# Decayed attention and a leaky-ReLU MLP on one core: loads of v on a second queue, more buffers for q, k and v, and a new order of all work

## The chip, the cores and the metric

The kernel runs on 1 core of one Trainium2 chip. The metric is device time in microseconds (us) of one execution; the median of the runs is given with the lowest and the highest. The engines are named as in the profile: PE (TensorE matmul), PEld (its weight loads), DVE (VectorE), ACT (ScalarE), POOL (GpSimd) and SP (SyncE, which only issues DMAs here). Each engine takes its instructions in the order in which they were written; engines wait for each other by semaphores.

## The reference

```python
# q, k, v: float32 [8 batches, 8 heads, 576 positions, 64]
scores = q @ k^T / sqrt(64)
gamma  = 1 - 2 ** (-5 - head)
ret    = scores * (gamma ** (i - j) where i >= j, else 0)
x      = (ret @ v), heads side by side     # [4608 tokens, 512]
h      = x @ w_in                          # [4608, 2048]
out    = max(0.01 * h, h) @ w_out          # [4608, 512], float32
```

## The kernel before

**Units and groups.** The 4608 tokens are 36 units of 128 tokens (`u` = 0 to 35), and four units make a group of 512 tokens (`g` = 0 to 8). The attention is done in linear form over chunks of 64 positions: a state (a sum of k^T v, with decay) is carried from chunk to chunk, so that a unit needs only its own scores and the state before it. Everything behind the loads is fp16 with float32 sums in PSUM.

**The jobs of a unit.** Each piece of work has a name:

- `ld{u}.1`, `ld{u}.0`, `ld{u}.2`: the loads of k, q and v, 256 KB each (L335 to L346), into `t32_1`, `t32_0`, `t32_2`; each of the three has `ld` = 4 buffers
- `ck`, `cq`, `cv`: casts to fp16, q and v with a decay factor (L364 to L385), into `qk16` and `v16`
- `tp{u}.x` with `yt{u}.x` (units 0 to 7): transposes of k (x = 1) and q (x = 0) on PE and their copy out of PSUM; `tr{u}` (units 8 to 35): the transpose of both by a DMA on SP's queue (L387 to L396). Both fill `qkT`
- `sb`: k^T v of the two chunks; `st{u}.j`: its sum into the state (DVE, an `s` at the end of the name for the step with decay); `sx`: the state's cast to fp16
- `sa`, `mk`: the scores and their masking on DVE; `oa` (units 0 to 3) or `ca` and `ow` (later ones, `ca` holding the scores too): the output's matmuls; `x{u}`: its copy into `xT`

**The MLP.** `h{g}.{f}.{t}` are the plain products of layer 1 for groups 0 and 1 (f: first of the 128-wide column blocks, t: first token), `l...` the leaky ReLU behind them. One such job is 4 to 16 matmuls. For groups 2 to 8, layer 1 is four sets `a{g}.{n}` of seven block products each instead of eight, and layer 2 is `b{g}` with seven products `p1` to `p7`, each in two parts (`seven`, L736). Their sums on other engines are `cA`, `u2`, `k5` (copies out of PSUM) and `11`, `12`, `21`, `22` (results). `xs`, `m`, `ws` and `wm` are sums of inputs and of weights on DVE, `so` the stores of the results. The four quarters of `w_in` (`wi0` to `wi3`) and of `w_out` (`wo0` to `wo3`) are cast to fp16 by the DMA that loads them, always on POOL's queue.

**The order.** `ORDER` (L113) is one list of all jobs. `Plan.emit` (L44) writes them out in that order, so it fixes each engine's own order and that of the DMA queues: SP's queue issues the loads of its units, the transposes and the stores in the order in which they stand there, and POOL's queue its loads. `@n` says which of four PSUM banks a product takes. `+n@b` (`filler`, L970) puts n idle products of 512 columns on PE. `ENGINE` (L82) says whether a cast or a copy runs on DVE or on ACT. `CFG["loads"]` (L71) says which queue loads a unit: POOL's for units 1 to 11 and for v of unit 0, SP's for units 12 to 35.

**Buffers.** `qk16`, `v16`, `qkT`, the states `s32` and `st16` come from one pool with `ap` = 4 buffers each (L272). A job that writes a buffer waits until its last readers of four units ago are done.

**The end.** The last layer-2 group (`seven` with `last=True`) keeps two banks for its first product; `b8.11` is copied out in three pieces x, y and z, and `so8.11x` and `so8.11z` are issued by ACT, the other stores by SP.

Of the kernel before, what the change touches and what calls it, by code (L numbers as in the profile page):

```python
# [33 lines left out]
class Plan:  # L34
# [49 lines left out]
    for eng, names in {  # L84
        "DVE": """
            ck0 cq0 sx0.0 yt0.0 cq1 sx0.1 cv1 cq2 sx1.0 yt2.1 ck3 cq3 yt3.1 cv3 sx2.1 yt3.0 cq4 cv4 x3 ck5 cq5
            cv5 yt5.1 cq6 sx5 cv6 cq7 ck7 cv7 yt7.0 yt7.1 sx7 x7 cq8 cv8 cq9 cq11 cv10 cv12 cq13 cv13 b1.u2 ck15
            cv14 cq15 cq16 cv16 ck17 sx15 cv17 cq17 cq18 ck18 cv18 sx18 cq19 cv20 a3.2.cA cq20 cq21 sx19 a3.2.u2
            cq22 cv21 cv22 sx20 ck23 cv23 cq23 cq24 cv24 cq25 ck25 cv25 cq26 cv26 cq27 x23 cv27 cv28 cq28 x24
            cv29 ck30 sx27 cq30 cv30 ck31 a5.2.u2 a5.3.cA cq32 ck32 a5.3.u2 cv32 cq31 cq33 cv33 sx31.1 a6.0.u2  # L90
            cv34 ck34 cq35 cq34 cv35 x31 a6.2.k5 sx33 sx34 x32 x33 a7.1.k5 b6.11 a7.2.u2 a7.2.k5 x34 a7.3.u2
            a7.3.k5 a8.0.u2 a8.0.k5 b7.u2 a8.1.k5 a8.2.cA b7.21 a8.3.u2
        """,
        "ACT": """
            cv0 yt0.1 x0 ck1 ck2 yt1.1 yt1.0 cv2 yt2.0 x1 sx1.1 sx2.0 x2 sx3.0 ck4 sx3.1 yt4.1 yt4.0 ck6 sx4.1
            x4 yt5.0 x5 yt6.0 yt6.1 sx6 b0.cA x6 ck8 b0.11 ck9 b0.u2 ck10 cq10 b0.k5 sx8.0 cv9 cq12 cv11 ck12
            sx9 x8 ck11 sx10 b1.cA b0.21 x9 ck13 sx11 b1.11 sx12 x10 x11 ck14 a2.0.cA b1.k5 a2.0.u2 a2.0.k5 cq14
            cv15 x12 a2.1.cA sx13.1 sx14 a2.1.u2 x13 a2.1.k5 ck16 a2.2.cA a2.2.u2 b1.21 a2.2.k5 sx16 x14 a2.3.cA
            x15 a2.3.u2 a2.3.k5 sx17.0 b2.cA a3.0.cA b2.11 a3.0.u2 a3.0.k5 a3.1.cA a3.1.u2 x17 cv19 b2.u2 x16
            a3.1.k5 ck19 b2.k5 ck20 ck21 a3.2.k5 b2.21 ck22 x18 a3.3.cA a3.3.u2 a3.3.k5 x19 b3.cA a4.0.cA b3.11  # L100
            sx21 ck24 a4.0.u2 a4.0.k5 x20 a4.1.cA a4.1.u2 sx22.1 a4.1.k5 x21 b3.u2 sx23 a4.2.cA a4.2.u2 b3.k5
            ck26 sx24 a4.2.k5 x22 a4.3.cA sx25 a4.3.u2 a4.3.k5 ck27 b3.21 a5.0.cA b4.cA ck28 a5.0.u2 a5.0.k5
            sx26.0 b4.11 ck29 a5.1.cA cq29 a5.1.u2 a5.1.k5 x25 sx28 b4.u2 a5.2.cA x26 sx29 b4.k5 a5.2.k5 cv31
            x27 sx30 a5.3.k5 ck33 b4.21 x28 a6.0.cA x29 a6.0.k5 sx32 b5.cA a6.1.cA b5.11 a6.1.u2 x30 a6.1.k5
            a6.2.cA b5.u2 a6.2.u2 b5.k5 ck35 a6.3.cA a6.3.u2 a6.3.k5 sx35.0 a7.0.cA a7.0.u2 a7.0.k5 b5.21
            a7.1.cA b6.cA a7.1.u2 a7.2.cA b6.u2 b6.k5 x35 a7.3.cA a8.0.cA b6.21 b7.cA b7.11 a8.1.cA a8.1.u2
            b7.k5 a8.2.u2 a8.2.k5 a8.3.cA a8.3.k5 b8.cA b8.u2 b8.k5 b8.21 b8.11x so8.11x b8.11y b8.11z so8.11z
# [937 lines left out]
```

## Time and profile before

| | |
|---|---|
| median of 3 runs | 279.4 us (279.18 to 280.1) |
| the profiled execution | 281.98 us |
| its span, first to last instruction | 280.1 us |
| granted TensorE clock | 1.00 throughout |
| instructions | 10055 |
| DMA moved | 50.05 MB; HBM read 36.81 MB, written 9.44 MB |

The page lists the DMAs by queue: q1 is that of SP, q0 that of POOL. The share is the time that their packets took on the 16 DMA engines.

```profile
q1 hardware_dynamic: 111984, 35.99, 56.7%
q0 software_dynamic: 6992, 13.11, 19.4%
```

And by issue, with the KB of one and the median us from its issue to its landing:

```profile
out_dram<-osb SPq DMA_DIRECT2D x16, 512.0 KB, 4.2
t<-in_k_dram SPq DMA_DIRECT2D x22, 256.0 KB, 4.2
t<-in_q_dram SPq DMA_DIRECT2D x22, 256.0 KB, 4.5
t<-in_v_dram SPq DMA_DIRECT2D x21, 256.0 KB, 4.6
t<-in_v_dram POOLq DMA_DIRECT2D x11, 256.0 KB, 7.3
```

How to read them: a line of a timeline gives start, duration, engine, line of the kernel, operation, output and input, and in brackets how long the engine had been idle before and who released it. `SPq` is SP's queue; its duration is that of the issue, not of the transfer. Durations of matmuls overlap, since they are pipelined.

### The profile page before, as it was taken

What the parts mean: (1) busy time and instruction counts of PE and PEld (TensorE: products, weight loads), DVE (VectorE), ACT (ScalarE), POOL (GpSimd) and SP (SyncE); (2) the same over time, 40 slices, a digit from 0 to 9 for tenths busy, and PEclk for the clock granted to TensorE, in tenths of its full rate; (3) what the DMA queues carried; (4) which work ended last, traced back from release to release, by engine and by line L of the source; (5) the groups of instructions that cost most, each with busy time, mean ns of one, the idle gap of its engine ahead of it and who ended that gap; (6) DMA issues with size and microseconds to landing.
All of it is one profiled execution on the core that took longest, in us unless ns stands there. A gap on an engine that the chain in (4) does not pass through costs nothing.

```text
span 280.1 us, 10055 instructions
## 1 busy us (share of the span) xinstructions
PE 267.9 (96%) x4337; PEld 224.6 (80%) x4337; DVE 230.2 (82%) x432; ACT 201.2 (72%) x431; POOL 38.2 (14%) x49
## 2 busy tenths in 40 slices
PE   6887999999999899999999999999999999999995
PEld 2554688888888788888887888888888888888884
...
GB/s 217 245 236 233 305 248 235 263 178 194 190 233 196 214 211 235 181 242 205 267 200 192 216 196 245 192 258 180 209 40 61 168 2 2 150 2 2 124 25 153
DMA packets 119597, 50.05 MB, mean 179 GB/s; under 512 B 107904, under 2 KB 113280, under 8 KB 119552
## 3 DMA queue, kind: packets, MB, share of 16 engines
q1 hardware_dynamic: 111984, 35.99, 56.7%
q0 software_dynamic: 6992, 13.11, 19.4%
...
q10 hardware_dynamic: 576, 0.31, 0.4%
...
HBM read 36.81 MB, written 9.44 MB: 165 GB/s over the span
## 4 chain that ended last, share of the span: by engine, by line
PE 85%; DMA 8%; DVE 2%; issue 2%; ACT 1%; POOL 1%; SPq 0%; ACTq 0%; POOLq 0%; DVEq 0%
PE acc L901 39%; PE acc L823 28%; PE acc L634 10%; DMA t<-in_k_dram 6%; PE ot L536 4%; DMA qkT<-qk 2%; PE sc L448 2%; PE sc L439 2%; PE acc L405 1%; POOL t L340 1%; ACT gt L843 0%; DVE s L481 0%; DVE sum L847 0%; ACT acc L765 0%; DVE u L773 0%
## 5 line engine op out<-in xcount | busy, mean ns | idle before, releaser
L901 PEld LDWEIGHTS <-gt 128*128 128x128 f16 x720 | 70.0, 98 | 8.3
L901 PE MATMUL acc<-w_out,gt 128*128 128x256 f16 x432 | 53.4, 273 | 0.0
L823 PEld LDWEIGHTS <-w_in 128*128 128x128 f16 x448 | 42.6, 98 | 6.0 <-issue 0.6
L843 ACT ACTIVATE gt<-acc 128x512 f16<-128x512 f32 x56 | 33.3, 601 | 14.8 <-PE acc L823 14.5
L901 PE MATMUL acc<-w_mix,gt 128*128 128x256 f16 x288 | 36.2, 273 | 0.0
L823 PEld LDWEIGHTS <-w_sum 128*128 128x128 f16 x336 | 32.4, 98 | 4.4 <-issue 0.4
L851 ACT ACTIVATE gt<-sum 128x512 f16<-128x512 f32 x56 | 34.4, 635 | 1.1 <-DVE sum L847 0.9
L823 PE MATMUL acc<-xs,w_sum 128*128 128x256 f16 x224 | 33.6, 273 | 0.4 <-DVE u L773 0.4
L823 PE MATMUL acc<-xs,w_in 128*128 128x256 f16 x224 | 33.3, 273 | 0.6 <-ACT gt L843 0.6
L823 PE MATMUL acc<-xT,w_in 128*128 128x256 f16 x224 | 33.6, 273 | 0.0
L634 PE MATMUL acc<-xT,w_in 128*128 128x256 f16 (+2 forms) x272 | 30.8, 266 | 0.2 <-ACT xT L585 0.2
L901 PEld LDWEIGHTS <-mix 128*128 128x128 f16 x288 | 27.8, 98 | 4.1 <-DVE mix L877 0.7
L454 DVE TENSOR_TENSOR s<-sc,cs 128x512 f16<-128x512 f32 x36 | 24.6, 684 | 6.3 <-PE sc L439 3.5
L634 PEld LDWEIGHTS <-w_in 128*128 128x128 f16 x272 | 22.1, 98 | 5.2 <-issue 0.4
L762 ACT COPY acc<-acc 128x512 f32<-128x512 f32 x33 | 19.0, 576 | 9.4 <-PE acc L901 4.2
L847 DVE TENSOR_TENSOR sum<-acc,k 128x512 f32<-128x512 f32 x28 | 19.2, 687 | 6.5 <-ACT k L776 3.5
L369 DVE TENSOR_TENSOR qk<-t,cs 128x512 f16<-128x512 f32 x32 | 21.9, 684 | 2.4 <-DMA t<-in_q_dram 2.3
L776 ACT COPY k<-acc 128x512 f32<-128x512 f32 x31 | 18.3, 589 | 7.2 <-PE acc L823 3.7
L641 ACT ACTIVATE gt<-acc 128x512 f16<-128x512 f32 x32 | 18.4, 597 | 6.4 <-PE acc L634 6.1
L585 ACT CAST xT<-ot 128x512 f16<-128x512 f32 x28 | 16.4, 592 | 8.9 <-PE ot L536 8.3
L847 DVE TENSOR_TENSOR sum<-acc,u 128x512 f32<-128x512 f32 x28 | 19.2, 686 | 2.7 <-ACT u L773 1.3
L773 ACT COPY u<-acc 128x512 f32<-128x512 f32 x27 | 16.0, 591 | 6.7 <-PE acc L823 3.4
...
## 6 DMA issues: line engine op xcount, KB each, us to landing
out_dram<-osb SPq DMA_DIRECT2D x16, 512.0 KB, 4.2
t<-in_k_dram SPq DMA_DIRECT2D x22, 256.0 KB, 4.2
t<-in_q_dram SPq DMA_DIRECT2D x22, 256.0 KB, 4.5
t<-in_v_dram SPq DMA_DIRECT2D x21, 256.0 KB, 4.6
t<-in_v_dram POOLq DMA_DIRECT2D x11, 256.0 KB, 7.3
t<-in_q_dram POOLq DMA_DIRECT2D x10, 256.0 KB, 8.9
t<-in_k_dram POOLq DMA_DIRECT2D x10, 256.0 KB, 7.4
w_in<-in_moe_w_in_dram POOLq DMA_DIRECT2D x4, 512.0 KB, 8.0
```

The costliest lines, as they stand in the source:

```text
L369: engine[e].tensor_tensor(out=view[0](out), in0=view[1](t32[u, 2 * x][:]), in1=view[1](decay(u, x)), op=MUL)
L454: landed[u] = nc.vector.tensor_tensor(out=s[:], in0=sc[:, :, 0], in1=mask_sb.unsqueeze(1).unsqueeze(1).to_broadcast([P, 2, NP, CH]), op=MUL,)
L585: moved[u] = copies[xe](out=x_of(u).rearrange("q c (j t) -> q j c t", j=2), in_=at)
L634: nc.tensor.matmul(out=a[:, n, :], lhsT=w_in16[:, c, (f0 + n) * P : (f0 + n + 1) * P], rhs=x[:, c, t0 : t0 + nt], start=(n == 0 and c == 0 ...
L641: nc.scalar.activation(out=y[:, f0 : f0 + nf, t0 : t0 + nt], in_=a[:], func=mybir.ActivationFunctionType.Lrelu)
L762: copies[ce](out=B[:], in_=A[:])
L776: op("k5", ke, lambda: copies[ke](out=k5[:], in_=C[:]), [done["5"]], [k5], [C])
L823: nc.tensor.matmul(out=r[:, f, :], lhsT=w[:, c, (2 * n + f) * P : (2 * n + f + 1) * P], rhs=rhs[:, c, :], start=fresh and c == 0 and f == ...
L843: w = op(what, "ACT", lambda: nc.scalar.activation(out=to(), in_=r[:], func=lr), after, [y], [r])
L847: what, "DVE", lambda: nc.vector.tensor_tensor(out=s[:], in0=r[:], in1=plus[:], op=ADD),
L851: f"l{g}.{n}.{what}", "ACT", lambda: nc.scalar.activation(out=to(), in_=s[:], func=lr), [j], [y],
L901: nc.tensor.matmul(out=(r[tb] if isinstance(r, tuple) else r)[:, tb, :], lhsT=lhs[n]()[:, f, tb * P : (tb + 1) * P], rhs=rhs[n][:, f, :], ...
```

## The change

It does four things.

1. v of units 12 to 35 is loaded by POOL's queue; q and k stay on SP's.
2. `qk16` gets 5 buffers and `qkT` 6, each from a pool of its own; `v16` has a pool of its own too, with 4 as before.
3. In the last layer-2 group the bank of products 5 and 3 (C) is no longer one of the four, but that of the scores, `sc`, which is free by then; product 5 waits for the last masking and the last states.
4. `ORDER` and `ENGINE` are written anew: places of all jobs, banks, fillers (33 idle products before, 43 after) and the engine of some 95 casts and copies.

```diff
@@ CFG
     ld=4,
     ap=4,
+    cp=5,
+    vp=4,
+    tp=6,
...
-        ("u", 12, "SP"), ("u", 13, "SP"), ("u", 14, "SP"), ("u", 15, "SP"), ("u", 16, "SP"), ("u", 17, "SP"),
+        ("u", 12, ("SP", "SP", "POOL")), ("u", 13, ("SP", "SP", "POOL")), ("u", 14, ("SP", "SP", "POOL")), ("u", 15, ("SP", "SP", "POOL")), ("u", 16, ("SP", "SP", "POOL")), ("u", 17, ("SP", "SP", "POOL")),
...
@@ ORDER, the beginning
-    ld0.1 ld0.2 ld0.0 ld1.0 ld1.1 ld2.1 ck0 ld2.0 cq0 ld1.2 cv0 cq1 ld2.2 +13@3 tp1.0@0 wi1 tp0.0@1 tp0.1@2 sb0 +4@3
-    yt0.1 ld3.1 st0.0 ck1 yt0.0 ld3.0 cq2 yt1.0 tp1.1@3 ck2 sa0 +3@0 cv1 ld4.1 yt1.1 st0.1 sx0.0 sb1 cv2 tp2.1@2
-    +2@0 mk0 ld3.2 sx0.1 sa1 tp2.0@1 ld4.0 st1.0 oa0 +7@0 mk1 x0 sx1.0 st1.1s yt2.0 yt2.1 sx1.1 sa2 sb2 oa1 +2@0
-    ld5.0 x1 ck3 wi2 st2.0 tp3.1@0 mk2 h0.6.0@3 +2@1 ld4.2 st2.1 ck4 cq3 l0.6.0 yt3.1 tp3.0@1 ld5.1 sx2.0 h0.4.0@2
-    yt3.0 cv3 ld5.2 sa3 oa2 cq4 sb3 wi3 x2 tp4.1@3 st3.0 mk3 l0.4.0 wi0 h0.4.256@0 sx3.0 sx2.1 cq5 ld6.0 oa3
-    l0.4.256 tp4.0@1 x3 tp5.0@2 ld6.1 st3.1s yt4.0 h0.11.0@0 sx3.1 ld6.2 h0.9.0@1 yt5.0 yt4.1 ld7.0 h0.10.0@2 ck5
+    ld0.1 ld0.2 ld0.0 ld1.1 ld1.2 ld1.0 ck0 wi0 ld2.2 cv0 cq0 ld2.0 +13@3 sb0 +1@0 tp0.0@0 cv1 ld2.1 tp0.1@1 +7@2
+    yt0.0 st0.0 ld3.0 st0.1 yt0.1 ck1 ld3.1 sx0.1 sb1 +5@0 st1.0 ld3.2 cq1 sx1.0 sx0.0 st1.1s tp1.0@2 +1@0 sa0
+    tp1.1@3 +14@0 mk0 yt1.0 ld4.1 yt1.1 cv2 sx1.1 ld5.1 ck2 wi1 cq2 tp2.1@0 sa1 ld4.2 yt2.1 oa0 sb2 x0 tp2.0@1 +2@0
+    st2.0 ck3 ld6.1 mk1 tp3.1@2 yt3.1 cv3 oa1 ld4.0 st2.1 h0.0.0@3 x1 cq3 yt2.0 ck5 ld5.0 sx2.0 sa2 ck4 sb3 tp3.0@0
+    mk2 ld5.2 tp5.1@2 yt3.0 st3.0 oa2 tp4.1@1 sa3 wi3 yt4.1 h0.6.0@0 x2 cv4 ld6.2 h0.0.128@1 yt5.1 l0.6.0 st3.1s
+    ld6.0 ck6 h0.0.256@2 mk3 sx3.0 wi2 l0.0.0 cq4 h0.4.0@0 l0.0.128 ld7.2 cq5 l0.0.256 sb4 tp4.0@3 ld7.1 sx3.1
+    tp5.0@1 sx2.1 cv5 oa3 ld7.0 st4.1 h0.4.256@2 x3 yt4.0 ld8.0 l0.4.0 ca4 l0.4.256 sb5 tp6.1@3 sx4.1 ld8.2
...
@@ ORDER, the end
-    b8.p1.0@1,0 so7.0 a8.3.12 l8.3.22 b8.p1.1 m8.0.0 l8.3.12 m8.1.0 a8.3.p4.0 b8.cA@2 m8.0.1 a8.3.21 b8.p6.0 m8.1.1
-    b8.p5.0@3 m8.2.0 m8.2.1 b8.p6.1 m8.3.1 b8.p5.1 b8.u2 m8.3.0 b8.p7.0 b8.k5 b8.p7.1 b8.p3.0 b8.22 b8.p3.1 so8.22
-    b8.p4.0 b8.12 b8.p4.1 so8.12 b8.p2.0 b8.21 so8.21 b8.p2.1 b8.11x so8.11x b8.11y b8.11z so8.11y so8.11z
+    a8.3.p6.0 m8.0.0 a8.3.p2.0 a8.3.u2 a8.3.p3.0 a8.3.11 a8.3.p7.0 a8.3.12 b7.21 b8.p5.0 l8.2.22 a8.3.22 so7.1
+    b8.p1.0@1,3 l8.3.12 m8.1.0 l8.3.22 b8.p1.1 m8.0.1 a8.3.p4.0 b8.cA@0 m8.1.1 b8.p5.1 a8.3.21 m8.2.1 b8.p6.0 m8.2.0
+    b8.k5 b8.p6.1 m8.3.1 b8.p2.0 b8.u2 b8.p7.0 b8.11x m8.3.0 b8.p7.1 b8.p3.0 b8.22 b8.p3.1 so8.22 b8.p4.0 b8.12
+    b8.p4.1 so8.12 b8.p2.1 b8.21 so8.21 b8.11y b8.11z so8.11y so8.11x so8.11z
...
@@ the pools and their users
     a_pool = pool("ap", CFG["ap"])
+    c_pool = pool("cp", CFG["cp"])
+    v_pool = pool("vp", CFG["vp"])
+    q_pool = pool("qp", CFG["tp"])
...
-        t = qk16[u] = Buf(a_pool, [P, 2, H, D], F16, "qk16", turn=u)
-        s = v16[u] = Buf(a_pool, [P, H, D], F16, "v16", turn=u)
+        t = qk16[u] = Buf(c_pool, [P, 2, H, D], F16, "qk16", turn=u)
+        s = v16[u] = Buf(v_pool, [P, H, D], F16, "v16", turn=u)
...
-        t = qkT[u] = Buf(a_pool, [P, 2, NP, P], F16, "qkT", turn=u)
+        t = qkT[u] = Buf(q_pool, [P, 2, NP, P], F16, "qkT", turn=u)
...
@@ seven
-        A, B, C = (bank(), bank()) if last else bank(), bank(True), bank()
+        A, B, C = (bank(), bank()) if last else bank(), bank(True), sc[:, 0].rearrange("p x c t -> p x (c t)") if last else bank()
+        idle_sc = [masked[NU - 1]] + states[NU - 1] + states[NU - 2] if last else []
...
-        product("5", C, True, [])
+        product("5", C, True, idle_sc)
```

The places of `tr15` and `ca15`, and of `ld27.1` and `ck27`, with what stands between them:

```diff
@@ ORDER, the middle
-    tr15 x13 ld18.2 st15.0s a2.2.p5.0@0 a2.2.cA@2 so1.0 a2.1.p4.0 cq16 a2.2.k5 a2.2.p2.0 a2.1.21 st15.1 a2.2.p6.0
-    mk14 a2.2.11 a2.2.p3.0 sx15 a2.2.u2 a2.3.p5.0@3 a2.3.p1.0@1 a2.2.12 a2.3.k5 a2.2.p7.0 tr16 ld18.1 cv17 a2.3.cA@0
-    ow14 ca15
+    tr15 ld17.0 b1.21 a2.1.p7.0 l2.1.12 ld18.1 a2.2.p5.0@0 a2.1.22 a2.2.cA@2 ld18.0 ow13 sb16 a2.2.k5 ca14 cv17
+    a2.2.p6.0 sx15 a2.1.p4.0 ld21.2 a2.2.u2 x13 a2.2.p3.0 a2.1.21 mk14 a2.2.p2.0 a2.2.p7.0 ck17 a2.2.11 a2.3.p1.0@1
+    a2.2.12 l2.1.22 a2.3.p5.0@3 a2.2.22 a2.3.cA@0 ow14 ca15
...
-    ld27.1 l4.1.22 st24.1 a4.2.p2.0 ld27.2 cv25 a4.2.p6.0 ld28.1 a4.2.11 m3.3.1 ow22 ca23 b3.k5 sb25 a4.2.p5.0@1 x22
-    mk23 b3.p3.0 sx24 b3.22 a4.2.u2 b3.p3.1 st25.0 a4.2.k5 cv26 l4.0.12 a4.2.p7.0 ck26 a4.2.p3.0 tr25 ld29.1 a4.2.22
-    ck27
+    ld27.1 a4.2.p7.0 a4.2.k5 b3.p5.0@1 st24.1 sx23 ck25 l4.0.22 b3.p5.1 x21 ck26 cv25 b3.p7.1 b3.k5 mk22 ld29.2
+    l4.1.22 a4.2.p3.0 a4.2.22 cq25 tr24 ld28.1 ow22 ca23 b3.22 sb25 b3.p3.0 st25.0 mk23 b3.p3.1 a4.2.12 sx24 cq28
+    b3.p4.0 b3.12 cq26 a4.3.p1.0@0 tr25 so3.0 b3.p4.1 cq27 ld29.0 a4.3.cA@1 st25.1 a4.2.p4.0 ck27
```

Between `ld30.1` and `ck30` stood 9 products of `a`, 2 half products of `b` and 3 of the small blocks `sb`, `ow` and `ca`; now it is 20, 6 and 8.

In `ENGINE`, of the work of units 8 to 31 and groups 0 to 5, these go from ACT to DVE: ck11 ck14 ck16 ck19 ck27 ck28, cq12 cq29, cv15 cv31, sx8.0 sx12 sx16 sx22.1 sx25, x17 x20 x21 x27, and the copies b0.k5 a2.0.u2 a2.2.u2 a4.0.u2 a4.3.u2 a5.0.u2 a5.1.k5 a5.2.k5. From DVE to ACT: ck15 ck18 ck23 ck30 ck31, cq11 cq25 cq28, cv13 cv14 cv29, sx15 sx18 sx27, x23 x24 x31, b1.u2 a3.2.cA a5.2.u2 a5.3.cA a5.3.u2. At the end b8.k5 and b8.11x go to DVE.

More of the change, by code (lines that the diff above doesn't have):

```diff
@@ L85 @@
         "DVE": """
[L86 to L90, printed above, removed]
@@ L91 @@
-            cv34 ck34 cq35 cq34 cv35 x31 a6.2.k5 sx33 sx34 x32 x33 a7.1.k5 b6.11 a7.2.u2 a7.2.k5 x34 a7.3.u2
-            a7.3.k5 a8.0.u2 a8.0.k5 b7.u2 a8.1.k5 a8.2.cA b7.21 a8.3.u2
+            cv0 ck0 cq0 yt0.1 cq1 ck1 ck2 sx0.1 yt1.1 cv1 yt1.0 cq2 cv2 sx1.1 ck3 cq3 cv3 sx2.1 sx3.1 cq4 cv4
+            yt4.0 ck5 cq5 cv5 yt5.1 cq6 yt5.0 sx5 cv6 cq7 yt6.0 yt6.1 ck7 cv7 sx7 x6 cq8 cv8 b0.k5 sx8.0 cq9
+            cq12 cv10 ck11 cv12 cq13 sx12 ck14 a2.0.u2 cv15 cq15 cq16 cv16 ck16 ck17 cv17 cq17 a2.2.u2 sx16 cq18
@@ L96 @@
[L96 to L105, printed above, removed]
@@ new lines @@
+            a2.1.u2 x13 a2.1.k5 sx15 a2.2.cA b1.21 a2.2.k5 x14 a2.3.cA x15 a2.3.u2 a2.3.k5 sx17.0 ck18 b2.cA
+            a3.0.cA b2.11 a3.0.u2 a3.0.k5 a3.1.cA sx18 a3.1.u2 cv19 b2.u2 x16 a3.1.k5 b2.k5 a3.2.cA ck20 ck21
+            a3.2.k5 b2.21 ck22 x18 a3.3.cA a3.3.u2 a3.3.k5 ck23 x19 b3.cA a4.0.cA b3.11 sx21 ck24 a4.0.k5
+            a4.1.cA a4.1.u2 a4.1.k5 b3.u2 cq25 sx23 a4.2.cA a4.2.u2 b3.k5 ck26 sx24 a4.2.k5 x22 a4.3.cA x23
+            a4.3.k5 b3.21 a5.0.cA b4.cA a5.0.k5 sx26.0 b4.11 cq28 x24 ck29 a5.1.cA cv29 a5.1.u2 x25 ck30 sx27
@@ L744, in product @@
                     f"{tag}p{n}.{i}", "PE", lambda n=n, r=r, fresh=fresh, i=i: mm(n, r, fresh, i),
-                    after + needs(n, i) + ([done[n, i - 1]] if i else []), whole(r), reads,
+                    after + needs(n, i) + ([done[n, i - 1]] if i else []), owned(r), reads,
                 )
```

191 lines of the change are left out of this document (100 added, 91 removed), and 6 rows, old and new, of the table loads.

## The prediction

> **What bounds the kernel now.** I read the summary of the page first, then the windows (busy time by stretch), then the list of waits on PE, then the timeline around each gap. In the first two fences the columns of a window are its length and the busy us of PE, PEld, DVE, ACT, POOL, then granted clock, DMA share and GB/s; a wait has its total us, count and longest.
>
> ```profile
> PE 267.9 (96%) x4337; PEld 224.6 (80%) x4337; DVE 230.2 (82%) x432; ACT 201.2 (72%) x431; POOL 38.2 (14%) x49
> ```
>
> ```profile
> 0.00:30.00 30.00, 23.52 (x417) 13.95 (x418) 17.66 (x39) 16.63 (x40) 24.64 (x34) 1.00 1.00 231
> 95.00:98.00 3.00, 1.97 (x76) 1.54 (x75) 2.43 (x5) 1.59 (x3) 0.00 (x0) 1.00 1.00 284
> 98.00:153.00 55.00, 55.00 (x990) 47.32 (x988) 52.11 (x101) 45.42 (x92) 0.00 (x0) 1.00 1.01 216
> 153.00:155.00 2.00, 1.38 (x14) 1.21 (x13) 1.97 (x5) 2.00 (x5) 0.00 (x0) 1.00 1.49 207
> 172.00:174.00 2.00, 1.59 (x70) 1.48 (x70) 1.84 (x4) 2.00 (x7) 0.00 (x0) 1.00 1.04 231
> 265.00:267.00 2.00, 1.66 (x17) 1.33 (x15) 1.93 (x4) 1.46 (x4) 0.00 (x0) 1.00 0.81 314
> 277.00:280.10 3.10, 0.00 (x0) 0.00 (x0) 0.00 (x0) 0.24 (x2) 0.00 (x0) 1.00 0.38 123
> ```
>
> ```profile
> PE acc L405 <- issue: 1.5, 1, 1.5
> ...
> PE ot L536 <- DMA qkT<-qk: 1.0, 1, 1.0
> PE acc L823 <- ACT gt L843: 0.6, 1, 0.6
> ...
> PE acc L823 <- DVE u L773: 0.4, 1, 0.4
> PE acc L901 <- ACT acc L765: 0.3, 1, 0.3
> ```
>
> PE bounds it. Of 280.1 us it is idle 12.2: 30 - 23.5 = 6.5 in the first 30 us, three gaps in the middle (1.03 + 0.62 + 0.41 = 2.06), 0.34 at 266, and 3.3 after its last matmul. The work on PE is the same after the change, at the same clock of 1.00, so only these gaps and the idle products (fillers, 33 before, 43 after, all in the opening) can pay. DMA is as full as PE until about 200 us (share 1.01 in the third row), and DVE has only 2.9 us free of those 55.
>
> **The middle.** Who made PE late there:
>
> ```profile
> 90.78 3.40 SPq L391 DMA_TRANSPOSE qkT<-qk  x1
> ...
> 97.06 0.25 PE L536 MATMUL ot<-qkT,st 64*64 64x64 f16 x6 [1.03 <-DMA qkT<-qk]
> ...
> 147.25 0.58 SPq L340 DMA_DIRECT2D t<-in_k_dram  x1
> ...
> 152.48 0.62 ACT L365 CAST qk<-t 128x512 f16<-128x512 f32 x1 [1.94 <-DMA t<-in_k_dram]
> ...
> 156.52 3.24 SPq L340 DMA_DIRECT2D t<-in_v_dram  x1
> ...
> 168.32 0.57 SPq L340 DMA_DIRECT2D t<-in_k_dram  x1
> ...
> 171.98 0.43 DVE L365 CAST qk<-t 128x512 f16<-128x512 f32 x1 [1.15 <-DMA t<-in_k_dram]
> ```
>
> By the order these are tr15 before ca15, ck27 on ACT (a4.2.21 stands behind it, whose bank a4.3.p5.0 waits for), and ck30 on DVE (a5.2.u2 behind it, on which product 7 waits). All three begin on SP's queue, which issues loads, transposes and stores one after the other:
>
> ```profile
> L391 SPq DMA_TRANSPOSE qkT<-qk x28: 1232/1600/3402, 55.8 to 218.7; - x28
> ```
>
> ```profile
> L369 DVE TENSOR_TENSOR qk<-t,cs x32: 673/684/693, 5.3 to 208.2; 128x512 f16<-128x512 f32 x32
> ...
> L340 SPq DMA_DIRECT2D t<-in_v_dram x27: 504/622/3242, 59.4 to 196.0; - x27
> ...
> L340 POOL DMA_DIRECT2D t<-in_v_dram x13: 697/884/1018, 1.3 to 46.1; - x13
> L365 DVE CAST qk<-t x13: 417/421/822, 3.8 to 200.2; 128x512 f16<-128x512 f32 x13
> ```
>
> The change takes 24 loads of v from SP: 24 x 0.62 = 15 us of issue, and on POOL they cost 24 x 0.88 = 21 us of an engine whose last load now starts at 46.1 us and that has nothing else to do. Behind a waiting v on POOL only later loads of v are queued. The transfer itself gets shorter too. GB/s in half microseconds from the start:
>
> ```profile
> GB/s 0 0 0 58 128 270 293 249 306 379 352 320 336 344 311 320 328 295 320 248 156 182 162 188 190 272 215 238 256 322 291 303 254 246 172 131 180 336 199 209
> ```
>
> From 5 to 9.5 us POOL's loads alone run at about 325 GB/s, against 216 in the third window, where nearly all is SP's. A 262 KB load then takes 0.81 us against 1.21, 24 of them some 10 us less of DMA that is full.
>
> The order sets how long before its use each transfer is issued. I count the PE work that stands between the two in ORDER, at 0.87 us for eight products of 256 columns and 0.2 to 0.3 for a small block of `sb`, `ow` or `ca`:
>
> ```profile
> 19.72 0.87 PE acc L634 x8
> ```
>
> ld27.1 to ck27 goes from 4.7 to 8.6 us, ld30.1 to ck30 from 6.4 to 16.0, tr15 to ca15 only from 3.7 to 4.9. Of 28 pairs tr/ca 13 had under 5 us before, and one of them held PE for 1.03; after it is 6 (units 10, 11, 15, 16, 19, 29). For the loads of k it was 2 under 5 us and is 1 (ck12, 4.0). So I leave 6/13 x 1.03 = 0.5 for transposes and 0.1 for loads: 2.06 - 0.6 = **1.5 us gained** (bounds 2.06, and a loss of 0.5 if two transposes are late by 1.03 and both other gaps stay by half). The fifth qk16 and the fifth and sixth qkT cost no instruction; without them an earlier tr would only wait for its slot.
>
> **The start.** Until 25 us the loads on POOL's queue set the pace, the casts behind them:
>
> ```profile
> 6.23 2.02 ACT L375 ACTIVATE v<-t,cs 128x64 f16<-128x64 f32 x8 [3.09 <-DMA t<-in_v_dram]
> ...
> 11.58 2.02 ACT L375 ACTIVATE v<-t,cs 128x64 f16<-128x64 f32 x8 [0.38 <-DMA t<-in_v_dram]
> ...
> 16.29 0.90 POOL L340 DMA_DIRECT2D t<-in_q_dram  x1 [2.60 <-DMA w_in<-in_moe_w_in_dram]
> 16.80 0.61 DVE L365 CAST qk<-t 128x512 f16<-128x512 f32 x1 [1.55 <-DMA t<-in_k_dram]
> ...
> 25.36 0.61 PE L405 MATMUL acc<-ident,qk 128*128 128x128 f16 x8 [1.52 <-issue]
> ...
> 25.92 0.43 DVE L365 CAST qk<-t 128x512 f16<-128x512 f32 x1 [0.48 <-DMA t<-in_k_dram]
> ```
>
> A weight quarter costs 4.7 us (v2 at 11.58 to wi1 at 16.29), or 3.4 by the later one (k3 at 16.80 to k5 at 25.92 holds wi2 and seven loads of 0.81). After the change the queue is v0 (6.2), k1 v1 q1 (+2.4), wi0 (+3.4 to 4.7), v2 q2 k2 (+2.4: 14.4 to 15.7), q3 k3 v3 k4 k5 (+4.1), wi1 (+3.4 to 4.7): **21.9 to 24.5**. PE reaches h0.6.0, the first that needs wi1, by way of DVE: from k2 it runs ck2, cq2, st2.0, ck3, mk1, cv3, st2.1, cq3, ck5, mk2, five of 0.42 (casts, and the states of L481) and five multiplies of 512 columns like cq's 0.68, 5.5 us, to 19.9 to 21.2; with some 0.7 of handoffs (an estimate, ten of 0.07) and oa2, tp4.1, sa3 behind mk2 (1.2, oa2 like oa3 below) that is 21.8 to 23.1. So wi1 decides, and the ten added fillers (2.2 us at 0.215 each, half of this 0.431 mean, which overlap counts double) lie in waits that the loads make:
>
> ```profile
> L481 DVE TENSOR_TENSOR s<-sc,s 128x256 f32<-128x256 f32 x40 | 16.7, 418 | 3.1 <-PE sc L448 1.9 <-PE sc L439 1.0
> ...
> L973 PE MATMUL acc<-idle 128*128 128x512 f16 x33 | 9.7, 431 | 1.2 <-DVE idle L310 1.2
> ```
>
> At 25.36 the old kernel has three blocks of layer 1 of 0.87 done, oa3 too. The new one has h0.0.0 and, from 21.9 or 24.5 on, 4.0 or 1.0 blocks more, and tp5.1 (0.2) but not oa3, which takes 0.7 by two rows of the chain:
>
> ```profile
> 23.15 0.31 PE ot L536 x24
> ...
> 23.58 0.30 PE ot L536 x8
> ```
>
> That is ahead by 1.2 or behind by 1.4. wi3 and wi2 follow with about half a microsecond to spare. I take **0**, bounds 1.2 gained and 1.4 lost, near the middle as neither quarter's row is the better one.
>
> **The end.** Product 5 of the last layer-2 group gets its bank from the scores, so b8.p5.0 runs before b8.p1.0 and covers sums that came late (0.34 at 266). m8.0.1 still follows l8.3.22 closely: I take **0.2 gained** (0 to 0.34). Its new waits, mk35 and the states of units 34 and 35, are for work some 40 us older. At the very end ACT issues two stores:
>
> ```profile
> 276.33 0.38 ACTq L952 DMA_DIRECT2D out_dram<-osb  x1
> 276.80 0.43 ACT L938 COPY osb<-acc 128x128 f32<-128x128 f32 x2 [0.50 <-PE acc L901]
> 277.27 0.34 ACTq L952 DMA_DIRECT2D out_dram<-osb  x1
> ```
>
> Before, so8.11x went out ahead of the last two copies; now it stands behind them and ahead of so8.11z, whose issue is 0.38 later: **0.4 lost** (0 to 0.4). The moves between DVE and ACT are off the path as long as both keep free time; DVE gets some 2.5 us more (rival 2).
>
> **Sum:** 0 - 1.5 - 0.2 + 0.4 = -1.3 us. The profiled execution took 281.98 us (span 280.1 and 1.9 around it), so it becomes 280.7; the median of the runs is 279.4, 2.6 lower, and I carry the same 1.3 over: **278.1 us**.
>
> **The rivals.** (1) *No change*: the gaps move rather than go. For it: 6 transposes still have under 5 us, tr15 among them, and a transpose holds SP 1.6 to 3.4 us whatever is queued; against it: the leads of k. With 0.6 of the 2.06 gained and the end's 0.4 lost, 279.2 to 279.6, say 279.4. The Trainium skill, "DMA: Bandwidth & Descriptors", section "Issuing engines are not separate DMA queues", speaks for this rival: a DMA issued elsewhere runs on the same 16 engines and saves only its issue time. By that rule the 10 us of DMA are not won; the rates quoted above disagree with it so far.
> (2) *DVE becomes the bound.* It has 2.9 us free of 55. Counting the moved names with 0.42 and 0.68, some 2.5 us come to it between 60 and 200 us, 0.9 in that window; and a cast on DVE took up to 822 ns against 421 in this trace. With 0.4 more at each of the 9 loads of v in the window (3.6) it needs 4.5: 1.6 late there, an estimated 2.2 with the neighbouring stretches, so 279.4 - 1.3 + 2.2 = 280.3. Against it: the median cast took 421 although POOL was issuing loads in most of the first 46 us. The Trainium skill, "SBUF — State Buffer", section "SBUF: two separate sides", names such a cause: DVE and GpSimd share a port pair, and one that holds it blocks the other.
> (3) *Slower, by the start*: PE takes its work in order, so if wi1 comes late everything behind h0.6.0 stands. With 4.7 us for every quarter wi1 is at 24.5, which loses 1.4, and wi3 and wi2 then come 1.3 later still each, with only 0.5 spare: 1.4 + 1.6 = 3.0. 279.4 - 1.3 + 3.0 = 281.1. It decides as soon as wi1 is past 23.1.
> (4) *All gaps go*: 2.06 + 0.34 at the middle and end, 1.2 at the start, 0.4 lost: 276.2.
>
> **Chances.** Forecast 0.47 (277.2 to 279.0 by itself), rival 1 0.20, rival 2 0.08, rival 3 0.15, rival 4 0.10. A measurement of this kernel can tell about 0.3% from no change, that is 278.56 and 280.24. Faster: 0.34 of the forecast, rival 4 and 0.03 of rival 1, 0.47. Slower: rival 3, 0.05 of rival 2 and 0.02 of rival 1, 0.22. The rest, 0.31, is within. Range 276.5 to 281.1: it leaves out most of rival 4 and half of rival 3.
>
> **What would show it.** Right: PE's waits at L536 and L823 between 50 and 200 us sum to under 1 us; SP's issues of loads fall near 0.6 us; PE starts wi1's block by 23 us; ACT's last store is issued 0.4 us later behind the last matmul. Wrong: a gap of over 1.5 us at L634 before 40 us (rival 3); DVE above 97% busy with PE waiting for it (rival 2); new waits for qkT (rival 1).

## The result, and the profile after

The changed kernel takes **281.47 us** (median of 20 runs, 279.78 to 285.89); the kernel before, on the same chip, 279.45 us (20 runs, 278.22 to 283.79). The ratio is 1.0062, with a 95% interval of 1.0033 to 1.0091: some 1.7 us slower (0.9 to 2.5), where 278.1 was forecast. The medians are of all runs, but this ratio and every ratio below leave out the slow runs, those more than 1.5% above the fastest run of the same kernel. The profiled execution took 280.70 us (span 278.9).

From the page of the changed kernel, its summary and its DMA queues (packets, MB, share of 16 engines' span):

```profile
PE 270.3 (97%) x4347; PEld 225.9 (81%) x4347; DVE 231.3 (83%) x437; ACT 199.7 (72%) x433; POOL 61.7 (22%) x76
...
q1 hardware_dynamic: 86976, 29.70, 51.8%
q0 software_dynamic: 8960, 19.40, 28.4%
```

The windows of the same execution (columns as in the prediction):

```profile
0.00:30.00 30.00, 25.27 (x423) 15.44 (x424) 19.19 (x43) 11.61 (x23) 24.95 (x34) 1.00 0.98 242
50.00:100.00 50.00, 50.00 (x894) 43.02 (x892) 46.70 (x89) 42.63 (x107) 7.78 (x9) 1.00 1.15 221
100.00:150.00 50.00, 50.00 (x877) 43.17 (x869) 48.52 (x95) 41.96 (x90) 7.78 (x9) 1.00 1.12 229
150.00:200.00 50.00, 50.00 (x874) 43.57 (x873) 47.18 (x89) 42.79 (x92) 5.80 (x7) 1.00 0.91 198
250.00:270.00 20.00, 20.00 (x186) 17.90 (x184) 11.78 (x20) 11.42 (x22) 0.00 (x0) 1.00 0.14 53
```

Read by itself, this page confirms the forecast. Its 280.70 us is even the 280.7 that was forecast for a profiled execution, but that is luck: this execution lies 0.8 us below the median of its own kernel. PE has no idle time at all from 50 to 200 us, the 2.06 us of gaps are gone, and the wait at 266 us is gone too (20.00 of 20). Yet the kernel is slower. So a comparison of one execution with one may mislead, and the first thing to find out is how executions of one and the same kernel differ.

### The profile page after: what moved, and what is told of

The parts are those of the page before. It is cut to its first block, busy times and chain, and to the rows that moved or that the text cites. A ratio compares the mean times of both kernels' runs of the same rounds, so it can differ in the third digit from the quotient of the medians.

```text
span 278.9 us, 10117 instructions
## 1 busy us (share of the span) xinstructions
PE 270.3 (97%) x4347; PEld 225.9 (81%) x4347; DVE 231.3 (83%) x437; ACT 199.7 (72%) x433; POOL 61.7 (22%) x76
## 4 chain that ended last, share of the span: by engine, by line
PE 89%; DMA 5%; POOL 2%; issue 1%; DVE 0%; ACT 0%; ACTq 0%; POOLq 0%
PE acc L911 39%; PE acc L833 32%; PE acc L640 9%; PE ot L542 4%; DMA w_in<-in_moe_w_in_dram 3%; DMA t<-in_v_dram 3%; POOL t L346 2%; PE sc L454 2%; PE sc L445 2%; PE sc L911 1%; PE acc L411 1%; POOL w_in L612 0%; DVE qkT L418 0%; ACT osb L948 0%; ACTq L962 0%
## 5 line engine op out<-in xcount | busy, mean ns | idle before, releaser
L346 POOL DMA_DIRECT2D t<-in_v_dram x40 | 34.2, 856 | 116.2 <-DVE v L375 61.4
L911 PE MATMUL acc<-w_out,gt 128*128 128x256 f16 x416 | 51.8, 273 | 0.0
L853 ACT ACTIVATE gt<-acc 128x512 f16<-128x512 f32 x56 | 33.4, 600 | 14.6 <-PE acc L833 12.8
L772 ACT COPY acc<-acc 128x512 f32<-128x512 f32 x34 | 19.7, 579 | 9.0 <-PE acc L833 4.7
L375 DVE TENSOR_TENSOR v<-t,cs 128x512 f16<-128x512 f32 x29 | 19.8, 683 | 4.3 <-DMA t<-in_v_dram 4.0
L786 ACT COPY k<-acc 128x512 f32<-128x512 f32 x30 | 17.5, 588 | 7.4 <-PE acc L833 5.0
L375 DVE TENSOR_TENSOR qk<-t,cs 128x512 f16<-128x512 f32 x31 | 21.0, 682 | 0.7 <-DMA t<-in_q_dram 0.7
L647 ACT ACTIVATE gt<-acc 128x512 f16<-128x512 f32 x32 | 17.7, 596 | 4.6 <-PE acc L640 4.6
```

The source lines that it names most:

```text
L346: engine[eng].dma_start(out=t[CH * j : CH * j + rows], in_=(q, k, v)[x][b, :, CH * w : CH * w + rows, :].rearrange("h t d -> t h d"),)
L375: engine[e].tensor_tensor(out=view[0](out), in0=view[1](t32[u, 2 * x][:]), in1=view[1](decay(u, x)), op=MUL)
L647: nc.scalar.activation(out=y[:, f0 : f0 + nf, t0 : t0 + nt], in_=a[:], func=mybir.ActivationFunctionType.Lrelu)
L772: copies[ce](out=B[:], in_=A[:])
L786: op("k5", ke, lambda: copies[ke](out=k5[:], in_=C[:]), [done["5"]], [k5], owned(C))
L853: w = op(what, "ACT", lambda: nc.scalar.activation(out=to(), in_=r[:], func=lr), after, [y], [r])
```

## The experiments

**Two more executions of each kernel** (before_again, after_again), with nothing edited.

> The kernel before, unchanged, for a second profiled execution. Theory S (the prediction read its gain from an execution of the kernel before that was itself late; the change loses at its start and end in every execution): this execution is near the median, span about 277.5 us, with under 1 us of PE idle between 50 and 270 us instead of 2.4, so the gaps that the change removes are mostly not there. Theory Q (gaps of about 2 us are usual before, and the change loses as much elsewhere, by irregular delays that the loads of v on POOL's queue bring): PE idle between 50 and 270 us is again 2 us or more.

> The changed kernel, unchanged, for a second profiled execution. Its first one had no PE idle between 50 and 275 us and a span of 278.9, 0.8 below its median. Theory S: what is late in a slower execution lies before 50 us, and there is still under 0.5 us of idle in the middle. Theory Q: a slower execution shows gaps of 1 us or more between 50 and 200 us behind loads of v or transposes.

Measured: before_again 278.49 us, after_again 283.16 us. Windows of before_again:

```profile
0.00:30.00 30.00, 25.57 (x421) 14.55 (x421) 18.48 (x41) 17.22 (x41) 24.41 (x33) 1.00 0.99 228
50.00:100.00 50.00, 50.00 (x897) 43.20 (x897) 46.48 (x87) 43.60 (x111) 0.00 (x0) 1.00 1.01 223
100.00:150.00 50.00, 50.00 (x888) 43.00 (x872) 47.68 (x93) 41.53 (x86) 0.00 (x0) 1.00 1.03 221
150.00:200.00 50.00, 50.00 (x875) 43.66 (x874) 47.83 (x92) 42.46 (x91) 0.00 (x0) 1.00 0.95 212
250.00:270.00 20.00, 19.66 (x181) 17.46 (x179) 11.91 (x20) 10.37 (x19) 0.00 (x0) 1.00 0.15 56
```

and of after_again:

```profile
50.00:100.00 50.00, 49.65 (x860) 42.55 (x858) 45.95 (x88) 41.74 (x106) 7.77 (x9) 1.00 1.10 219
100.00:150.00 50.00, 49.88 (x891) 42.84 (x888) 48.42 (x94) 41.95 (x88) 7.79 (x9) 1.00 1.09 219
150.00:200.00 50.00, 49.14 (x877) 42.74 (x864) 46.23 (x86) 42.89 (x93) 5.79 (x7) 1.00 1.03 198
```

The picture is turned round: the old kernel has no gap in the middle, the new one has 1.33 us (0.35 + 0.12 + 0.86), most of it before a transposed q, as in the old kernel's first execution. For before_again this is what theory S forecast, under 1 us of idle. For after_again it is the sign of theory Q that came, over 1 us behind transposes. So whether a kernel shows gaps differs from one execution to the next, for either order.

**A third and a fourth execution of before** (before_third; before_same, which was also timed against itself).

> The kernel before, a third profiled execution. Theory F (the gaps of the middle belong to some executions): between 50 and 200 us PE waits less than 1 us in all in one or two of the three executions, and where waits appear they stand at other instructions than in the first. Forecast's reading (the three gaps of 1.03, 0.62 and 0.41 us belong to the order and come each time): the same three waits again, 2 us in all.

> The kernel before, unchanged, timed against itself, to see what such a comparison scatters. All theories: ratio 1.000, within 0.997 to 1.003. If it comes out beyond 1.005 or under 0.995, differences of 1 to 2 us between other kernels of this study mean nothing.

Measured: before_third 279.27 us, idle 0.50 in the middle; before_same 1.71. The list of waits on PE in before_same between 50 and 200 us:

```profile
PE acc L823 <- DVE sum L847: 0.6, 1, 0.6
PE ot L536 <- DMA qkT<-qk: 0.6, 1, 0.6
PE acc L823 <- ACT gt L843: 0.5, 1, 0.5
```

The last of these stands at the same matmul as the 0.62 of the first execution (152.64 us here, 153.65 there), and the first is one that before_third has too (0.36 there). The transpose that is late is another one. So an order has its own places at which PE can be late, and an execution shows some of them.

Timed against itself, the kernel before gave a ratio of 0.9961 (0.9929 to 0.9992): an identical program came out 0.4% apart, with an interval that leaves out 1. So a ratio within 0.4% of 1 shows nothing here, and even 0.5% carries little without a trace beside it.

With old_end (below; identical to the changed kernel up to its last store) the executions can be set side by side. The middle is 150 us less PE's busy time in the three windows. The start is PE's busy time in the first 30 us less that of the idle products, all of which lie there, so it is the useful work done by then. The last column is the same for the first 23.2 us:

| execution | time, us | PE idle 50 to 200 | useful work by 30 us | by 23.2 us |
|---|---|---|---|---|
| before, the one in the prediction | 281.98 | 2.07 | 23.52 - 9.7 = 13.8 | 8.6 |
| before_again | 278.49 | 0 | 25.57 - 10.9 = 14.7 | 8.5 |
| before_third | 279.27 | 0.50 | 25.53 - 10.6 = 14.9 | 8.6 |
| before_same | 280.41 | 1.71 | 25.75 - 11.1 = 14.7 | 8.6 |
| changed | 280.70 | 0 | 25.27 - 12.1 = 13.2 | 7.5 |
| after_again | 283.16 | 1.33 | 25.68 - 13.0 = 12.7 | 6.9 |
| old_end | 280.57 | 0.99 | 26.49 - 12.8 = 13.7 | 7.0 |

Middle: 1.07 in the mean before, 0.77 after, 0.3 gained, which is far less than executions of one kernel differ. Start: 14.5 against 13.2 by 30 us, **1.3 lost**. Each of the three new executions lies below each of the old, if narrowly (13.7 against 13.8); against the one in the prediction alone it would be 0.6. By 23.2 us the two are further apart, 8.6 against 7.1, because PE has then not yet come to a stop that some executions have behind that point (last section). Seven executions of kernels below that have one of the two starts as it stands, at a granted clock of 1.00, agree: 8.2 to 9.0 by 23.2 us in the five with the old start, 6.5 and 7.0 in the two with the new one (new_start, v_on_sp).

**The start alone** (new_start): the kernel before with the first 330 entries of the new order and their engines.

```diff
-ORDER = before
+ORDER = after[:330] + [job for job in before if job not in after[:330]]
```

> The kernel before with the first 330 entries of the order, their engines, banks and 43 fillers taken from the changed kernel; from about 65 us on, and in queues, buffers and end, it is the kernel before, with all of q, k and v of units 12 to 35 on SP's queue. Theory S: the start alone costs 0.9 us or more, 1.003 to 1.006. Theory Q: no loads of v on POOL's queue after unit 11, so 0.999 to 1.002.

Measured: 280.84 us, ratio 1.0044 (1.0007 to 1.0081). Its window and its group of idle products (busy us, mean ns | idle before):

```profile
0.00:30.00 30.00, 25.06 (x431) 15.56 (x431) 19.80 (x43) 11.86 (x23) 25.01 (x34) 1.00 0.97 242
```

```profile
L971 PE MATMUL acc<-idle 128*128 128x512 f16 x43 | 11.9, 419 | 1.2 <-DVE idle L308 1.2
```

25.06 - 11.9 = 13.2, just as in the changed kernel. The time is 1.2 us longer (0.2 to 2.3). After before_same such a ratio alone would show little; with the 13.2 beside it, the start's loss comes with the order of the start, and costs about what it measures.

**The start undone** (old_start, old_start2, old_start3): the changed kernel with the first 317, 316 or 222 entries of the old order; in the last two the store of `so8.11x` is issued early as well.

```diff
-ORDER = after
+ORDER = before[:317] + [job for job in after if job not in before[:317]]
```

> The changed kernel with the first 317 entries of the order, their engines, banks and 33 fillers taken from the kernel before; from about 65 us on, and in queues, buffers and end, it is the changed kernel. Theory S: the start's loss of about 0.9 us is gone and the middle stays free of gaps, only the later last store (0.4) is left: 0.996 to 1.000 of the kernel before. Theory Q: the delays by v on POOL's queue stay, 1.004 to 1.007.

> The changed kernel with the first 316 entries of the order before (with their engines), one fewer than in the run named old_start, so that the cast of v of unit 12 no longer stands ahead of mask 9; and the store of the last group's third quarter issued right behind its copy. Theory F: no 1.17 us gap at 69 us, the start as in the kernel before, the last matmul to the end of the span 3.6 to 3.8 us instead of 4.15: 279.3 to 280.3 us, ratio 0.998 to 1.004. Theory Q: the middle still loses 1 to 2 us in the mean against the kernel before: 280.8 to 281.8 us, ratio above 1.004.

> The changed kernel with the first 222 entries of the order before, which end at about 45 us, where fewer jobs of the two orders lie crosswise than at 316; and the store of the last group's third quarter issued right behind its copy. Theory F (1.3 us lost at the start, 0.5 at the end): PE busy without idle products in the first 30 us some 14.5 us instead of 13.1, the last matmul to the end of the span 3.75 instead of 4.15, and, if the seam costs nothing, 279.2 to 280.2 us, ratio 0.997 to 1.003. Rival (the new middle loses too, whatever stands ahead of it): above 280.6, ratio above 1.004, with PE waiting over 1 us between 50 and 200 us.

Measured: 281.78, 283.21 and 283.83 us, ratios 1.0073 (1.0031 to 1.0116), 1.0106 (1.0065 to 1.0147) and 1.0117 (1.0075 to 1.0159). The start came back (24.76 - 10.3 = 14.5 in old_start), but all three times lie above what theories S and F forecast (1.004 at most). Each seam made waits of its own: PE waited 1.2 us for a masking on DVE in old_start, and up to 2.0 for a transpose in the other two. So these times neither confirm nor refute that the start is the loss. They do say that pieces of two such orders don't add up.

**Why the start loses** (wi0_later, wi0_later2). The timelines of DVE and of PE in the changed kernel:

```profile
15.09 0.43 DVE L371 CAST qk<-t 128x512 f16<-128x512 f32 x1 [0.68 <-DMA t<-in_k_dram]
```

```profile
12.37 3.18 PE L983 MATMUL acc<-idle 128*128 128x512 f16 x14
15.61 0.38 PE L411 MATMUL acc<-ident,qk 128*128 128x128 f16 x4
...
19.07 1.07 PE L640 MATMUL acc<-xT,w_in 128*128 128x128 f16 x16
```

k of unit 2 lands late, PE covers it with 14 idle products. The edit moves the weight quarter that stands ahead of it, and shortens the cover:

```diff
-    ... ck0 wi0 ld2.2 cv0 cq0 ld2.0 ... ld2.1 ... tp1.1@3 +14@0 mk0 ...
+    ... ck0 ld2.2 cv0 cq0 ld2.0 ... ld2.1 wi0 ... tp1.1@3 +3@0 mk0 ...
```

(wi0_later2 keeps 9 idle products there and has 6 for 2 ahead of unit 3.)

> The changed kernel with the first quarter of w_in issued behind the three loads of unit 2 instead of ahead of them, and 3 idle products instead of 14 in the wait that unit 2's k made. Theory F: k of unit 2 lands about 3.4 us earlier (the cast that starts at 15.09 us starts at 11.5 to 13), PE comes to its first layer-1 block 1 to 3 us earlier, and what is gained is kept until the second quarter of w_in decides (22 to 24 us): the time falls by 0.5 to 1.5 us against the changed kernel, to 280.0 to 281.0. Rival (the second quarter of w_in, which keeps its place in the queue, sets PE's pace alone): PE starts the block that needs it at 22.5 to 23.5 us as before and the time stays at 281.2 to 281.8.

> As the run wi0_later, with 9 idle products instead of 3 in the wait ahead of unit 2 and 6 instead of 2 ahead of unit 3, so that PE doesn't stand idle there and the granted clock stays near 1.00 in the first 30 us. Theory K (the late k of unit 2 is what costs the start 1.2 us): PE starts the block of the second quarter of w_in by 22 us, and the time falls to 280.2 to 280.9. Theory L (VectorE's chain of work and unit 3's k decide, so k of unit 2 is no more than the first of several): the block starts at 22.6 us or later and the time stays at 281.2 to 282.0.

Measured: wi0_later 281.91 us, ratio 1.0091 (1.0056 to 1.0126). PE's timeline in it:

```profile
14.64 0.40 PE L408 MATMUL acc<-ident,qk 128*128 128x128 f16 x4 [1.63 <-DVE qk L368]
...
18.00 0.40 PE L408 MATMUL acc<-ident,qk 128*128 128x128 f16 x4 [1.31 <-DVE qk L368]
...
19.36 1.89 PE L637 MATMUL acc<-xT,w_in 128*128 128x128 f16 x16
```

The cast came only 0.9 us earlier, because DVE was busy until then, and PE, left idle twice, did its first layer-1 block in 1.89 us instead of 1.07; the granted clock of the first 30 us was 0.94 (0.50 from 18.9 to 22.2 us). The run told more of idle products than of k.

wi0_later2: 283.07 us, ratio 1.0107 (1.0055 to 1.0159). PE starts the block of wi1 at 22.55, between what theories K and L forecast. By 30 us its useful work is 27.14 - 12.7 = 14.4, as much as before, but by 23.2 us it is not:

```profile
0.00:23.20 23.20, 20.45 (x320) 10.96 (x321) 14.68 (x32) 7.81 (x15) 19.49 (x28) 1.00 0.98 253
0.00:30.00 30.00, 27.14 (x470) 16.55 (x471) 19.85 (x45) 12.84 (x25) 25.91 (x35) 1.00 1.00 247
```

20.45 - 12.7 = 7.7, against 7.1 after and 8.6 before. The rest of the recovery is that PE did not stop behind that point in this execution. So the late k and its cover account for some 0.6 of the 1.5 us that are lost by 23.2 us; what makes the other 0.9 is not shown. The time is not better, and neither theory forecast that. DVE's timeline and PE's list of waits say what is late next:

```profile
57.46 0.69 DVE L683 TENSOR_TENSOR w_mix<-w_out 128x1024 f16<-128x1024 f16 x1 [2.88 <-DMA w_out<-in_moe_w_out_dram]
```

```profile
PE acc L908 <- DVE w_mix L683: 1.7, 1, 1.7
```

PE comes 1.7 us too early for the weight sums of layer 2, whose w_out quarter lands at 57.4; in the changed kernel it landed at 56.5, and DVE waited 0.2 us for it. In this execution the queue of weights on POOL is the next limit, right behind the start.

**The queue alone, from both sides** (v_on_sp, old_order). v_on_sp is the changed kernel with the old list of loads, old_order the old order and engines with the new queues and buffers:

```diff
-    ("u", 12, ("SP", "SP", "POOL")), ... ("u", 35, ("SP", "SP", "POOL")),
+    ("u", 12, "SP"), ... ("u", 35, "SP"),
```

> The changed kernel with v of units 12 to 35 back on SyncE's queue; order, engines and buffers as changed. Theory F (the loss is fixed: about 1.3 us in the first 30 us and 0.5 us at the end; the queue of v does little in the middle, because the gaps of the middle come in some executions of either kernel): the first 30 us and the end are the same as in the changed kernel, so no gain: 281.0 to 282.5 us, ratio to the kernel before 1.003 to 1.011. Theory Q (v on GpSimd's queue is what makes the middle irregular): the middle loses its gaps, the time falls to the start's and the end's loss alone at most, below 280.8 us. Theory P (the forecast's own: 15 us less issue on SyncE and 10 us less DMA are worth a gap of 1 us or more): without them it is slower than the changed kernel by 1 us or more, above 282.5 us.

> The order and the engines of the kernel before, with the changed kernel's queues (v of units 12 to 35 by GpSimd) and its buffers (5 qk16, 4 v16, 6 qkT). Theory G (the queue gains by itself, in either order; the run v_on_sp showed it worth some 2.5 us in the new one): 1 us or more faster than the kernel before, 277.0 to 278.5 us, ratio 0.991 to 0.996, and no wait of PE over 0.5 us between 50 and 200 us. Theory R (the queue only pays for what the new order loses: that order was made for v on GpSimd, and the old one leaves SyncE enough time): within 0.7 us of the kernel before, 279.0 to 280.2, ratio 0.998 to 1.002. Either way the first 30 us and the end are as in the kernel before.

Measured: v_on_sp 284.43 us, ratio 1.0142 (1.0097 to 1.0186); old_order 280.12 us, ratio 1.0026 (0.9990 to 1.0062). By these times the queue is worth some 2 us in the new order (1.0142 against 1.0062), and nothing in the old one. Theory F missed in v_on_sp, and theory P, the forecast's own, had the right size there. But theory G, which carries that gain to the old order, missed in old_order: the queue does not gain by itself. Theory Q, that v on GpSimd's queue makes the middle irregular, falls too. What comes nearest is theory R, that the queue only pays for what the new order loses. Where v_on_sp loses is not shown: its profiled execution, 281.83 us, was the shortest of its six. The longest entry among the waits on PE in old_order between 50 and 200 us shows that relief for SP doesn't end these gaps:

```profile
PE ot L539 <- DMA qkT<-qk: 1.8, 2, 1.6
```

The traces show what becomes of the relief. There are nine traced executions with the old order behind the start and nine with the new. PE waited for the transpose of unit 15 (tr15 in the prediction) in four of the old, 0.2 to 1.2 us, and in none of the new. In its place it waited for that of unit 26 in four of the new, 0.5 to 1.0 us, and in none of the old. Issue of tr26 on SP and the end of PE's wait, in old_end and in v_on_sp:

```profile
153.34 2.56 SPq L394 DMA_TRANSPOSE qkT<-qk  x1
...
164.66 0.25 PE L539 MATMUL ot<-qkT,st 64*64 64x64 f16 x6 [0.99 <-DMA qkT<-qk]
```

```profile
160.00 1.31 SPq L397 DMA_TRANSPOSE qkT<-qk  x1
...
165.35 0.25 PE L542 MATMUL ot<-qkT,st 64*64 64x64 f16 x6 [0.72 <-DMA qkT<-qk]
```

With v on POOL's queue SP issues tr26 6.7 us earlier, but it takes 11.3 us to land (10.9 in after_again) instead of 5.3. The slowest transpose of an execution took 6.1 us from issue to landing in v_on_sp and 6.3 to 7.0 in the four of before, but 8.9 in the changed kernel, 16.7 in after_again and 16.5 in old_end (old_order: 7.2). So what SP's issue gains is paid back in the landing. What slows the landing is not isolated.

**The end** (old_end, new_end, new_end2). old_end is the changed kernel with one entry moved; new_end and new_end2 are the kernel before with product 5 of the last group ahead of product 1, new_end with separate pools, new_end2 with the old one.

```diff
-    ... b8.11x m8.3.0 ... so8.11y so8.11x so8.11z
+    ... b8.11x so8.11x m8.3.0 ... so8.11y so8.11z
```

> The changed kernel with one entry of the order moved: the store of the last group's third quarter stands right behind its copy on VectorE, not behind the last two copies on ScalarE. By the forecast's own step 0.4 us of the change's loss goes: from the last matmul to the end of the span 3.75 us instead of 4.15, and 281.0 us instead of 281.5. Rival (the last store lands when the DMA before it does, whatever ScalarE issues first): 4.1 us again and no difference.

> The kernel before, its queues, buffers and order, with only one part of the new end: product 5 of the last layer-2 group stands ahead of product 1, in the bank of the scores, and the first sum that it needs right behind the last leaky ReLU that it reads. By the forecast's step (0.2 us gained, 0 to 0.34) the wait of 0.34 us near 266 us goes and nothing new comes: 20.00 busy us of PE between 250 and 270 us instead of 19.66, and 279.2 us instead of 279.5, which is below what the times can tell. Rival: the wait moves to product 1 or to the sums behind it, 19.66 again.

> The kernel before with the new place of product 5 and its sum at the end, and the old single pool. Theory M: the loss of new_end was the pools', so here 279.0 to 279.7 us, ratio 0.997 to 1.002. Theory E (product 5 in the bank of the scores costs it): 280.5 us or more, ratio above 1.005, with the waits of new_end behind 250 us.

Measured: old_end 280.75 us, ratio 1.0073 (1.0044 to 1.0102); new_end 281.25 us, 1.0085 (1.0052 to 1.0117); new_end2 280.65 us, 1.0023 (0.9991 to 1.0056). The last work of PE and ACT in the changed kernel, from its timelines:

```profile
274.03 1.04 PE L911 MATMUL acc<-w_out,gt 128*128 128x256 f16 x8
```

```profile
275.10 0.27 ACT L948 COPY osb<-acc 128x128 f32<-128x128 f32 x1 [0.29 <-PE acc L911]
275.11 0.37 ACTq L962 DMA_DIRECT2D out_dram<-osb  x1
275.26 0.27 ACT L948 COPY osb<-acc 128x128 f32<-128x128 f32 x1
275.57 0.43 ACTq L962 DMA_DIRECT2D out_dram<-osb  x1
```

and in old_end:

```profile
274.20 1.04 PE L908 MATMUL acc<-w_out,gt 128*128 128x256 f16 x8
```

```profile
275.28 0.43 ACT L945 COPY osb<-acc 128x128 f32<-128x128 f32 x2 [0.29 <-PE acc L908]
275.74 0.34 ACTq L959 DMA_DIRECT2D out_dram<-osb  x1
```

From the end of the last matmul to the end of the span it is 278.9 - 275.07 = 3.83 us in the one and 278.7 - 275.24 = 3.46 in the other: the moved store costs 0.37. The last store is issued 0.50 us after the last matmul in both; what differs is the issue of `so8.11x`, 0.46 us ahead of `so8.11z` in the one and 6.1 in the other (0.94 in the kernel before). That the two stores slow each other down is argued from this, not shown. The loss itself comes each time: 3.6 to 3.9 us behind the last matmul in the six executions that end with the stores of the changed kernel, 3.1 to 3.6 in the nine with those of before. The wait of 0.34 at 266 us did not go in new_end2 (19.45 of 20 between 250 and 270), so it takes more of the new end than that one product. In the changed kernel it is gone.

**The pools** (split_pools). new_end came out slower with nothing but the pools changed before 250 us, so these were tried alone.

```diff
-    t = qk16[u] = Buf(a_pool, [P, 2, H, D], F16, "qk16", turn=u)
+    t = qk16[u] = Buf(c_pool, [P, 2, H, D], F16, "qk16", turn=u)
... (v16 and qkT likewise)
```

> The kernel before with pools of their own for qk16, v16 and qkT, 4 buffers each as before: order, queues, counts and every instruction stay, only the places in SBUF differ. Theory M (the places cost the middle): 280.5 to 281.5 us, ratio 1.005 to 1.010, with waits of 1 to 2 us in all on PE between 90 and 200 us. Theory F (only start and end cost; the places are free): ratio 0.997 to 1.003.

Measured: 279.89 us, ratio 0.9990 (0.9957 to 1.0022). Separate pools cost nothing. Why new_end, in its six runs, took 2 us more than before stays open; its waits stood in the middle, where executions scatter.

## Why the prediction was wrong, step by step

**"The middle", 1.5 gained, and "I carry the same 1.3 over": the first step that failed.** The rows were read rightly, but 1.5 us of gaps were taken out of an execution of 281.98 us and the result then off the median of 279.4, as if every run had those gaps. Of 123 runs of the kernel before, with a median of 279.51, ten took 281.98 us or more. In its four traced executions the gaps are 2.07, 0, 0.50 and 1.71, so the median held about 1 us to win, not 2, and 0.77 is still there after: 0.3 gained, where 1.5 was forecast, and with this scatter 0.3 can't be told from nothing. The step's own remark that the median lies 2.6 lower was the warning. Its count of leads failed too: it looked for transposes with under 5 us between issue and use. The wait for tr15 did go, but tr26, which was not among the six that it named, came late though issued 10 us ahead of its use.

**The 15 us of issue on SP** were relieved as worked out (24 loads at 0.6), and the sign "SP's issues of loads near 0.6" came true (medians of 0.591 for k, 0.626 for q). It did not end the late transposes: old_order waits 1.8 us for them with the relief.

**The 10 us less of DMA** did not come. A share times the span is time of all 16 engines. For q1 (SP's queue) and q0 (GpSimd's) together this is 217.2 us in the mean of the four executions of before (213 to 221), and 226.5 in three of after (with old_end). The two runs that change the queue alone, old_order and v_on_sp:

```profile
q1 hardware_dynamic: 86976, 29.70, 51.0%
q0 software_dynamic: 8960, 19.40, 27.4%
```

```profile
q1 hardware_dynamic: 111984, 35.99, 62.3%
q0 software_dynamic: 6992, 13.11, 19.6%
```

In the old order, moving v gives 220.0 us instead of 217.2; in the new order 226.5 instead of 229.4. Each difference is smaller than the scatter of before, so the queue saves the engines nothing that these runs can tell. The new order adds some 6 to 12 us of that time, and why is not shown. The forecast's 1.21 came from a window that holds transposes and stores as well, its 0.81 from a stretch in which nothing else ran. The rule of the Trainium skill that the forecast held against itself ("DMA: Bandwidth & Descriptors", "Issuing engines are not separate DMA queues") was right: these four sums agree with it.

**"The start", taken as 0** (1.2 gained to 1.4 lost), lost 1.3: the second step that failed, and as large as the first. The path was right: PE started the block of wi1 at 22.83, by 23 as forecast and without a wait for wi1 (after_again: 23.49). By 25.36 the new kernel was even a little ahead of the execution it was compared with (useful work 9.6 us against 9.2). But that execution had stood 1.52 us in "issue" just then. The forecast counted the two orders at the one moment at which this stall had taken the old one's lead away: by 23.2 us, ahead of the stall, the new kernel is 1.1 us behind the same execution, and 1.5 in the mean of the table. The product behind that stall, at 25.36 there, starts at 24.54 in before_again and at 24.53 in before_same, and the new kernel met such a stall itself, 0.98 us, right after 25.36 (last section).

**"The end", 0.2 gained and 0.4 lost:** 0.34 gained, 0.37 to 0.5 lost (3.83 us against 3.30 in before_same). Right in size; the reason given for the loss, a later issue, was not the one. ACT issues its last store 0.50 us behind the last matmul in either kernel, so the sign "issued 0.4 us later" did not come.

The terms as measured are 1.3 - 0.3 - 0.34 + 0.5 = 1.2 us slower, inside the 0.9 to 2.5 of the times; the first two come from a few executions each and are no better than that. Of the rivals, the third forecast 281.1 us by a late start; that is the time, but not by its mechanism, as wi1 held nobody. The first, that gaps move rather than go, is what happened in the middle: from unit 15 to unit 26. The second did not come: DVE was busy 48.52 of 50 us from 100 to 150, and PE waited for nobody there. The sign "waits between 50 and 200 us under 1 us" was fulfilled in the changed kernel's first execution and meant nothing, as before_again fulfils it too.
